# Forgetting attention with a feed-forward network on one core: exponentials transposed in 32 by 32 blocks by VectorE and carried across partitions by wide DMAs, in place of TensorE transposes

## The chip, the cores and the metric

The kernel runs on one core of a Trainium2 chip. The metric is the time of the core in microseconds (us), from the first to the last instruction and what lies around them. Engines: TensorE (PE, with its weight loads PEld), VectorE (DVE), ScalarE (ACT), GpSimd (POOL), SyncE (SP), whose queue issues all DMAs here. SBUF is the working memory with 128 partitions, PSUM the eight banks that TensorE writes.

## The reference, cut to what matters

```python
scores = scale * np.matmul(q, k.transpose(0, 1, 3, 2))       # q, k, v: 8 batches, 8 heads, 576 tokens, 64
cum = np.cumsum(np.log(np.clip(f, 0.0001, 1.0)), axis=-1)
decay = cum[:, :, :, None] - cum[:, :, None, :]
scores = np.where(causal, -1000000000.0, scores + decay)     # causal: above the diagonal
attn = np.exp(scores - np.max(scores, axis=-1, keepdims=True))
attn = attn / (np.sum(attn, axis=-1, keepdims=True) + 1e-09)
x = np.matmul(attn, v)                    # then tokens by heads: 4608 x 512
h = x @ w_in                              # 512 x 2048
out = np.maximum(0.01 * h, h) @ w_out     # 2048 x 512
```

All is float32. The kernel gets float32 precision by splitting each operand into a high part, rounded to the type fp32r that TensorE multiplies in one pass, and a low part, the rest.

## The kernel before, in words

A first stage, called early here, handles the first 256 tokens of batches 0, 1 and 2 and loads and splits the weights of the feed-forward network. Then comes the main loop over 64 tasks, one a head: batches 3, 4, 5, 6, 7 whole (tasks 0 to 39, all 576 rows; "whole heads"), then the remaining rows 256 to 575 of batches 0, 1 and 2 (tasks 40 to 63; "short heads").

A head is worked in row blocks i = 0 to 4 (a short one in blocks 2 to 4). `scores` multiplies the split q and k (tiles s1, s2 stationary, m1, m2 moving, into PSUM banks `sc`), VectorE adds the causal mask and takes the row maximum (L425), ScalarE takes the exponential with the row sum (L431) into tile z of the block. The exponentials then stand with rows on partitions, but the product with v needs the columns there. One head later, `transposes` turns each 128-column piece by a TensorE matmul against the identity (L447) into PSUM `tr`; ScalarE rounds it to the high part `ph` (L460), VectorE subtracts to the low part `pl` (L462). `values` multiplies with the split v (`vs`, L489), adds the two halves of the result (L496, L497) into x. For each pair of heads, `inverse` takes reciprocals of the row sums, turns them on TensorE and spreads them over partitions through DRAM (`inv`, `rb`); `normalise` multiplies x by them (L530) and writes x to the DRAM tensor `xd`.

The feed-forward network takes groups of 256 tokens from `xd` as they become ready. It is a generator, `ffn`, which yields after each quantum of TensorE work: 12 matmuls of the first product (L576, banks `h`) or 6 of the second (L614, banks `o0`, `o1`); 576 quanta in all. `fill(step)` draws quanta between the parts of a head, so that TensorE works on them while the other engines handle scores; `step` is set from the quanta available (`have`) and the tasks left until the next batch is ready. The activated g is rounded on VectorE (L589) and its low part taken on GpSimd (L140).

The order of each engine's instructions is mostly that of a scheduler that moves instructions by its own estimates; only those given to `keep_in_program_order` keep the written order. Semaphores tie the engines; tiles of one tag share buffers, so a later one waits for the readers of an earlier one.

Of the kernel before, what the change touches and what calls it, by code (L numbers as in the profile page):

```python
# [16 lines left out]
P = 128  # L17
DELAY = 3
ORDER = (3, 4, 5, 6, 7, 0, 1, 2)
HP = 4  # L20
# [3 lines left out]
B2 = 7  # L24
# [9 lines left out]
ZE = (("z0", "z1", "z2", "z3"), ("vm", "s2b", "m2b", "s2a"))  # L34
# [3 lines left out]
WARM = (20, 2)  # L38
NEG = -1.0e30
REBIAS = 2.0**-112  # L40


@with_exitstack
def forgetting_attention_ffn(ctx, tc, qT, kT, v4, vr, f, w_in, w_out, out):
# [6 lines left out]
    nc = tc.nc  # L51
# [8 lines left out]
    STEP = (P + REST) // 2  # L60
    ST = [*range(0, (NFULL - 1) * P + 1, P)]
    ST.append(ST[-1] + STEP)
# [5 lines left out]
    PST = S - P  # L68
    PT0 = NFULL * PST + STEP
    PTW = PT0 + P  # L70
# [7 lines left out]
    def rows(i):  # L78
        return P if i < NFULL - 1 else STEP

    def width(i):
        return ST[i] + rows(i)

# [35 lines left out]
    make_identity(nc, eye)  # L119
# [72 lines left out]
    def decays():  # L192
# [8 lines left out]
        d = one.tile([P, P + T], F32, tag="z3", name="d")  # L201
        for i in range(2):
            n = width(i)
# [31 lines left out]
    def load(t):  # L235
# [4 lines left out]
        for name, src, lo in (("q", qT, a), ("k", kT, 0)):  # L240
            x = h[name] = one.tile([P, S], F32, tag=f"{name}raw", name=f"{name}raw_{t}")
            for o in range(2):
                nc.sync.dma_start(x[o * D:(o + 1) * D, lo:n], src[s][:, lo:n])
        if s % 2 == 0:
# [4 lines left out]
            pairs[s // 2, c0] = dict(vm=vm)  # L249

    early = {}

    def early_load(b, g):

        e = early[b, g] = {}
        x = e["qk"] = one.tile([P, 2, T], F32, tag="b2", name=f"qk_{b}_{g}", bufs=B2)
# [4 lines left out]
        v = e["v"] = one.tile([P, 2, T // P, D], F32, tag="b2", name=f"ve_{b}_{g}", bufs=B2)  # L261
        nc.sync.dma_start(v, v4[b * HPB // 2 + g][:, :, :T // P])

    def early_split(b, g, mx, sm):
# [13 lines left out]
        for i in range(2):  # L278
            n, at = width(i), i * P
# [20 lines left out]
    def early_scores(b, g):  # L300
# [38 lines left out]
    def early_values(b, g):  # L339
        e = early[b, g]  # L340
        out = psum.tile([P, 512], F32, tag="tr", name=f"ave_{b}_{g}")
        for o in range(2):
# [5 lines left out]
            pt = one.tile([P, 3 * P], F32, tag=("z4", "m2a")[o], name=f"pte_{b}_{g}_{o}")  # L348
# [15 lines left out]
    def fix():  # L364

        for x in "ab":
# [4 lines left out]
            y = fixed["sum" + x] = one.tile([P, NCH, 2], F32, tag="sum" + x, name=f"fixed_sum{x}")  # L371
            nc.gpsimd.memset(y, 1.0)
        for i in range(NFULL - 1, NCH):
            z = fixed[f"z{i}"] = one.tile([P, (i + 1) * P], F32, tag=f"z{i}", name=f"fixed_z{i}")
            nc.gpsimd.memset(z, 0.0)
        vs = fixed["vs"] = one.tile([P, 2, NCH, 2 * D], F32R, tag="vs", name="fixed_vs")
        vm = fixed["vm"] = one.tile([P, 2, NCH, D], F32, tag="vm", name="fixed_vm")
        nc.gpsimd.memset(vm[:, :, NFULL], 0.0)

    def split(t):  # L380
# [5 lines left out]
        x = "ab"[t % 2]  # L386
        s1 = h["s1"] = one.tile([P, S], F32R, tag="s1", name=f"s1_{t}", bufs=1)
        m1 = h["m1"] = one.tile([P, S], F32R, tag="m1", name=f"m1_{t}", bufs=1)
        s2, m2 = h["s2"], h["m2"] = fixed["s2" + x], fixed["m2" + x]
        nc.scalar.copy(s1[:, a:n], h["q"][:, a:n])  # L390
        nc.scalar.copy(m1[:, :n], h["k"][:, :n])
        nc.sync.dma_start(s2[D:, a:n].bitcast(F32), s1[D:, a:n].bitcast(F32))
        nc.sync.dma_start(s2[2:4, a:n].bitcast(F32), dec_q[s][:, a:n])
        nc.sync.dma_start(m2[:2, :n].bitcast(F32), dec_k[s][:, :n])
        minus(s1[:D, a:n], h["q"][:D, a:n], s1[:D, a:n].bitcast(F32))
        minus(m2[D:, :n], h["k"][D:, :n], m1[D:, :n].bitcast(F32))
# [362 lines left out]
```

## Time and profile before

| | |
|---|---|
| median of 3 runs | 1197.04 us (1196.57 to 1198.4) |
| profiled execution | 1197.86 us, its span 1196.1 us |
| PE, PEld busy | 99%, 88% |
| DVE, ACT, POOL busy | 49%, 53%, 36% |
| DMA | 110.48 MB, 30.4% of 16 engines |
| granted TensorE clock | 1.0 |

In rows of groups the columns are the line, engine, operation, tiles written and read, shapes and count, then busy us in all, mean ns of one, and the engine's idle time before with what ended it. In rows by time they are start, length, engine, line. In rows by stretch they are length, then busy time and instructions of each engine, TensorE's clock, the DMA engines' share and GB/s. A row of one line's instructions gives minimum, median and maximum in ns. Records of matmuls overlap, since they are pipelined.

### The profile page before, as it was taken

The numbers are of one execution on the slowest core, as the hardware profiler recorded it, in microseconds if no ns is written. First come the engines' busy times: TensorE is split into PE (matmuls) and PEld (weight loads), VectorE is DVE, ScalarE is ACT, GpSimd is POOL, SyncE is SP. The second block draws the span as 40 slices with busy tenths as digits, with TensorE's granted clock in tenths as the row PEclk, the third lists the DMA queues.
The fourth block names the chain that finished last, engine by engine and source line by source line (L and its number), as shares of the span: only waits on it lengthen the run. The fifth ranks groups of instructions, "written<-read, shape, count | busy, mean of one in ns | idle before, by whom it ended". The sixth has DMA issues, their size and how long they took to land.

```text
span 1196.1 us, 21843 instructions
## 1 busy us (share of the span) xinstructions
PE 1178.5 (99%) x7876; PEld 1050.5 (88%) x7876; DVE 581.3 (49%) x1561; ACT 636.2 (53%) x1531; POOL 436.6 (36%) x347
## 2 busy tenths in 40 slices
PE   9999999999999999999999999999999999999998
PEld 6777888989999989999989999999999899888987
DVE  6888655644545455444454354433343445552221
ACT  7877666755565555555565454433444556652111
POOL 1001534444535344444444443434343444441000
PEclk9999999999999999999999999999999999999999
DMA  7555333333233323333222223122212233321000
GB/s 235 192 182 187 88 118 98 92 115 89 80 99 98 116 68 92 98 106 86 73 87 91 88 67 100 48 76 74 76 55 88 69 101 100 90 69 55 11 18 18
DMA packets 75819, 110.48 MB, mean 92 GB/s; under 512 B 14464, under 2 KB 45424, under 8 KB 75712
## 3 DMA queue, kind: packets, MB, share of 16 engines
q1 hardware_dynamic: 75712, 109.09, 30.4%
q8 instruction: 62, 1.02, 0.3%
q14 instruction: 45, 0.37, 0.1%
HBM read 82.62 MB, written 18.56 MB: 85 GB/s over the span
## 4 chain that ended last, share of the span: by engine, by line
PE 89%; DVE 4%; ACT 3%; issue 2%; POOL 1%; DMA 0%; SPq 0%; DVEq 0%; ACTq 0%; POOLq 0%
PE h L576 32%; PE o L614 31%; PE av L489 8%; PE sc L420 8%; PE tr L447 6%; PE warm L115 1%; DVE wt L170 1%; POOL xs L140 1%; PE ave L351 1%; PE sce L313 1%; ACT ze L296 1%; ACT wt L167 1%; PE tre L345 0%; DVE fixed_z L425 0%; DMA rb<-inv 0%
## 5 line engine op out<-in xcount | busy, mean ns | idle before, releaser
L576 PE MATMUL h<-xh,win_h 128*128 128x256 f32 x1152 | 326.6, 284 | 0.8 <-DVE xh L548 0.8
L576 PE MATMUL h<-xh,win_l 128*128 128x256 f32 x1152 | 323.2, 281 | 0.0
L576 PE MATMUL h<-xs,win_h 128*128 128x256 f32 x1024 | 287.0, 280 | 4.6 <-POOL xs L140 4.6
L140 POOL TENSOR_TENSOR gl<-g,gh 128x512 fp32r<-128x512 f32 x116 | 150.3, 1296 | 319.7 <-DVE gh L589 297.1
L614 PE MATMUL o<-wout_h,gh 128*128 128x512 f32 x576 | 232.8, 404 | 0.0
L614 PE MATMUL o<-wout_l,gh 128*128 128x512 f32 x576 | 229.1, 398 | 0.0
L614 PE MATMUL o<-wout_h,gl 128*128 128x512 f32 x576 | 228.0, 396 | 0.0
L576 PEld LDWEIGHTS h<-xh,win_h 128*128 128x128 f32 x1152 | 217.1, 189 | 7.0 <-DVE xh L548 1.2
L576 PEld LDWEIGHTS h<-xh,win_l 128*128 128x128 f32 x1152 | 216.9, 188 | 0.3 <-issue 0.2
L583 ACT ACTIVATE g<-h 128x512 f32<-128x512 f32 x144 | 85.6, 594 | 220.3 <-PE h L576 219.9
L576 PEld LDWEIGHTS h<-xs,win_h 128*128 128x128 f32 x1024 | 193.0, 188 | 9.9 <-POOL xs L140 6.0
L460 ACT CAST ph<-tr 128x128 fp32r<-128x128 f32 (+2 forms) x272 | 121.7, 449 | 123.5 <-PE tr L447 120.6
L589 DVE CAST gh<-g 128x512 fp32r<-128x512 f32 x144 | 80.2, 557 | 218.1 <-ACT g L583 214.8
L140 POOL TENSOR_TENSOR s<-qraw,s 64x576 fp32r<-64x576 f32 (+1 forms) x64 | 78.9, 1233 | 268.2 <-ACT s L390 264.9
L462 DVE TENSOR_TENSOR pl<-tr,ph 128x128 fp32r<-128x128 f32 (+2 forms) x272 | 138.2, 516 | 42.5 <-ACT ph L460 42.4
L425 DVE CUSTOM_DVE_ANT_0 z<-sc,tri 128x128 f32<-128x128 f32 (+1 forms) x144 | 63.7, 444 | 142.0 <-PE sc L420 141.0
L614 PEld LDWEIGHTS o<-wout_h,gl 128*128 128x128 f32 x576 | 108.4, 188 | 24.6
L614 PEld LDWEIGHTS o<-wout_h,gh 128*128 128x128 f32 x576 | 108.7, 189 | 16.8 <-issue 0.2
L614 PEld LDWEIGHTS o<-wout_l,gh 128*128 128x128 f32 x576 | 108.7, 189 | 15.7
L420 PE MATMUL sc<-m,s 128*128 128x128 f32 (+2 forms) x336 | 121.6, 367 | 0.1
L431 ACT ACTIVATE fixed_z<-fixed_z,max 96x480 f32<-96x480 f32 (+1 forms) x128 | 94.3, 737 | 43.8 <-DVE max L425 42.5
L425 DVE CUSTOM_DVE_ANT_0 fixed_z<-sc,tri 96x480 f32<-96x480 f32 (+1 forms) x128 | 70.4, 550 | 75.9 <-PE sc L420 75.1
(129 smaller groups left out, 1826.5 us busy)
## 6 DMA issues: line engine op xcount, KB each, us to landing
kraw<-in_kT SPq DMA_DIRECT2D x128, 144.0 KB
qraw<-in_qT SPq DMA_DIRECT2D x80, 144.0 KB
wraw<-in_w_in SPq DMA_DIRECT2D x16, 512.0 KB
wraw<-in_w_out SPq DMA_DIRECT2D x16, 512.0 KB
fixed_vm<-in_v SPq DMA_DIRECT2D x32, 256.0 KB
xs<-xd SPq DMA_DIRECT2D x16, 512.0 KB
out<-ost SPq DMA_DIRECT2D x28, 256.0 KB
rb<-inv SPq DMA_DIRECT2D x40, 144.0 KB
```

The source lines that it names most:

```text
L140: nc.gpsimd.tensor_tensor(out, a, b, op=ALU.subtract)
L420: nc.tensor.matmul(ps[:m, :b - a], h["s" + w][:, cols], h["m" + w][:, a:b], start=y == 0, stop=y == 1,)
L425: nc.vector.tensor_tensor_reduce(out=z[:, a:b], in0=ps[:m, :b - a], in1=tri[:m, at:at + b - a], scale=-SCALE, scalar=3.0e38 if x == 0 else ...
L431: nc.scalar.activation(z, z, AF.Exp, bias=h["max"][:m, last:last + 1], scale=-1.0, accum_out=fixed["sum" + "ab"[s // 2 % 2]][:m, i, s % 2: ...
L447: nc.tensor.transpose(ps[:, x * m:(x + 1) * m], z[:m, j * P:(j + 1) * P], ident[:m, :m])
L460: nc.scalar.copy(o, src)
L462: nc.vector.tensor_tensor(o, src, hi.bitcast(F32), op=ALU.subtract)
L489: nc.tensor.matmul(ps[:, a - lo:hi - lo], fixed["vs"][:, odd, j, :], h[w][:, at:at + hi - a], start=(n == 0), stop=(n == len(steps) - 1),)
L576: nc.tensor.matmul(ph[:, e, :], w[:, c, fs], xx[:, c, :], start=(c == 0 and x == 0), stop=(c == NCC - 1 and x == 2),)
L583: nc.scalar.activation(g, ph, AF.Prelu, alpha=0.01)
L589: nc.vector.tensor_copy(gh, g)
L614: nc.tensor.matmul(acc[k], gg[:, e, ts], w[:, e, :], start=(fc_ == 2 * p0 and x == 0), stop=(fc_ == 2 * p1 - 1 and x == 2),)
```

## The change

The TensorE transposes go. VectorE transposes each block's exponentials within 32 by 32 squares (`turn`, eleven instructions a whole head) into a collecting tile `zt`. What is left of the transposition is a permutation of groups of 32 partitions: `send` writes `zt` to a DRAM tensor `zd` by DMAs of 32 partitions each (four after block 2 and four after block 4; four in a short head), and in the next head `receive` reads it back by one DMA of 128 partitions into `pl`. `divide` rounds it to `ph` on ScalarE and leaves the low part in `pl` on VectorE, in two halves. `values` runs two heads after `scores`. Row blocks now end at multiples of 128 counted from row 64, so that the first has 64 rows; the columns of `values` are in a permuted token order, which `segments` undoes when the output is written.

Beside this: s2 and m2 are made by `prepare`, with ScalarE casting the upper halves, in place of a DMA that copied a half of s1; loads run two heads ahead; `inverse` and its spreading are apart; g has 5 buffers in place of 7 and a yield moves ahead of its rounding; and from the main loop on, all five engines keep the written order (`Lanes`). With `LEAD`, the first tasks draw at least 7 quanta each while fewer than 48 are used. Every call now passes through one helper, so that most instructions bear one line number.

The diff, cut to its core:

```diff
-B2 = 7
+LEAD = 7
+B2 = 5
+        def issue(*args, **kw):
+            ins = f(*args, **kw)
+            if self.on[0]:
+                self.tc.keep_in_program_order(ins)
+            return ins
...
-    ST = [*range(0, (NFULL - 1) * P + 1, P)]
-    ST.append(ST[-1] + STEP)
+    ST = [0, *range(REST, S, P)]
+    Q = 32
+    FW, PW = 15 * Q, 12 * Q
...
+    def prepare(t):
...
+        for y, x, lo in ((s2, h["q"], a), (m2, h["k"], 0)):
+            nc.scalar.copy(y[D:, lo:n], x[D:, lo:n])
+        minus(h["q"][D:, a:n], h["q"][D:, a:n], s2[D:, a:n].bitcast(F32))
+        minus(m2[D:, :n], h["k"][D:, :n], m2[D:, :n].bitcast(F32))
...
-        nc.sync.dma_start(s2[D:, a:n].bitcast(F32), s1[D:, a:n].bitcast(F32))
...
-    def transposes(t, i):
-        for x, j in enumerate(blocks_):
-            nc.tensor.transpose(
-                ps[:, x * m:(x + 1) * m], z[:m, j * P:(j + 1) * P], ident[:m, :m]
-            )
...
+    def turn(t, i):
...
+            nc.vector.transpose(
+                ap(zt[0][:m], base + u * Q, *dims), z[:, js[0] * P:(js[-1] + 1) * P]
+            )
+        base, w, u = unit(t, i, i)
+        nc.vector.transpose(ap(zt[0][:m], base + u * Q, [w, 2]), z[:, i * P:i * P + 2 * Q])
+
+    def send(t, part):
...
+        src = src.rearrange("p (b c) -> p b c", b=4)
+        for a in range(4):
+            to = zd[t % 2][a, :, lo:hi].rearrange("(b i) c -> i b c", b=4)
+            nc.sync.dma_start(to, src[a * Q:(a + 1) * Q])
+
+    def receive(t):
+        w = PW if tasks[t][1] else FW
+        zq = state[t]["pl"] = one.tile([P, 4 * FW], F32R, tag="pl", name=f"pl_{t}")
+        y = zd[t % 2][:, :, :w].rearrange("a p c -> p a c")
+        nc.sync.dma_start(zq[:, :4 * w].bitcast(F32).rearrange("p (a c) -> p a c", a=4), y)
+
+    def divide(t, half):
...
+        z, ph = h["pl"][:, c], h["ph"][:, c]
+        nc.scalar.copy(ph, z.bitcast(F32))
+        nc.vector.tensor_tensor(z, z.bitcast(F32), ph.bitcast(F32), op=ALU.subtract)
...
                 nc.scalar.activation(g, ph, AF.Prelu, alpha=0.01)
+                yield True
                 gh = one.tile([P, 2, T], F32R, tag="b2", name=f"gh_{n}_{p}", bufs=B2)
...
-                yield True
                 if pending is not None:
...
+    for t in range(nt + 2):
+        if t < nt:
+            load_v(t)
...
         step = min(have / (left + SLACK), MAXQ) / 8
-        fill(step)
+        if used[0] < 3 * HP * (2 + T // P):
+            step = max(step, LEAD / 8)
         for i in range(5):
-            if i in before:
-                transposes(t - 1, i)
             if i in now:
                 scores(t, i)
+            if i - 1 in now:
+                spread(t, i - 1)
+            if old is not None and i == 0:
+                divide(old, 1)
+            if i == 0 and 0 < t <= nt and tasks[t - 1][0] % 2:
+                spread_inverse(t - 1)
+            if i == 1 and t + 1 < nt:
+                prepare(t + 1)
             fill(step)
+            if old is not None and i == 2:
+                values(old, 0)
...
+            if i == 2 and 0 < t <= nt:
+                receive(t - 1)
...
+                    add(old, part)
+                if s % 2:
+                    normalise(old)
...
+        if t + 2 < nt:
+            load(t + 2)
+        if t < nt:
+            spread(t, 4)
+            if tasks[t][0] % 2:
+                inverse(t)
+        fill(step)
+        if t < nt:
+            split_v(t)
+        fill(step)
+        if 0 < t <= nt:
+            divide(t - 1, 0)
+        fill(step)
```

How the order moves, at three places in the whole heads. First SyncE's queue over one head without an inverse; before (`fixed_s2`, `fixed_m2` are s2 and m2, `dec_q` and `dec_k` their decay rows in DRAM; the names end in the head and a number):

```order
L521 DMA rb_19_5243<-inv_126 64x576 x2
L393 DMA fixed_s2a_1527<-dec_q_128 2x576
L392 DMA fixed_s2b_1535<-s1_21_5352 64x576
L243 DMA qraw_22_5376<-in_qT 64x576 x2
L243 DMA kraw_22_5379<-in_kT 64x576 x2
L247 DMA fixed_vm_1548<-in_v4 128x2x256
L532 DMA xd_125<-x_18_5113 128x576
L248 DMA fixed_vm_1548<-in_vr 64x2x64
L394 DMA fixed_m2a_1530<-dec_k_127 2x576
```

And now:

```order
L54 DMA xs_6_5136<-xd_125 128x4x256
L54 DMA fixed_s2a_1466<-dec_q_130 2x576
L54 DMA fixed_m2a_1469<-dec_k_129 2x576
L54 DMA pl_20_5215<-zd_0_127 128x4x480
L54 DMA zd_1_128<-zt_1482 32x4x192 x4
L54 DMA xd_125<-x_18_5006 128x576
L54 DMA qraw_23_5271<-in_qT 64x576 x2
L54 DMA kraw_23_5274<-in_kT 64x576 x2
L54 DMA zd_1_128<-zt_1482 32x4x288 x4
```

The copy of a half of s1 is gone; the receive stands ahead of the first four sends of the head itself, and the loads, now for two heads later, stand between the two groups of sends.

Then VectorE from block 2 to block 4 of one head; before (ISA rows with `sc` are the mask and maximum, those without are the read of the maximum):

```order
L425 ISA z2_17_4639,max_17_4592<-sc_17_2_0_4640,tri_141 128x384
L425 ISA max_17_4592 128x1
L462 TENSOR_TENSOR pl_16_4586<-tr_16_2_4633,ph_16_4585 128x3x128
L425 ISA fixed_z3_1543,max_17_4592<-sc_17_3_0_4658,tri_141 96x480
L425 ISA max_17_4592 96x1
L462 TENSOR_TENSOR pl_16_4586<-tr_16_3_4651,ph_16_4585 128x4x96
L425 ISA fixed_z4_1545,max_17_4592<-sc_17_4_0_4684,tri_141 96x288
L425 ISA max_17_4592 96x1
L462 TENSOR_TENSOR pl_16_4586<-tr_16_4_4676,ph_16_4585 128x5x96
L425 ISA fixed_z4_1545,max_17_4592<-sc_17_4_1_4688,tri_141,max_17_4592 96x288
L425 ISA max_17_4592 96x1
```

And now:

```order
L54 ISA z3_21_5217,max_21_5128<-sc_21_3_0_5218,tri_144 128x448
L54 ISA max_21_5128 128x1
L54 STREAM_TRANSPOSE zt_1482<-z2_21_5178 128x2x4x32
L54 STREAM_TRANSPOSE zt_1482<-z2_21_5178 128x2x32
L54 TENSOR_TENSOR x_18_5006<-av_19_0_5197,y_19_5208 64x512
L54 TENSOR_TENSOR x_18_5006<-av_19_1_5210,yz_19_5213 64x64
L54 TENSOR_TENSOR x_18_5006<-x_18_5006,rb_19_4952 128x512
L54 TENSOR_TENSOR x_18_5006<-x_18_5006,rb_19_4952 128x64
L54 ISA z4_21_5241,max_21_5128<-sc_21_4_0_5242,tri_144 128x288
L54 ISA max_21_5128 128x1
L54 ISA z4_21_5241,max_21_5128<-sc_21_4_1_5246,tri_144,max_21_5128 128x288
L54 ISA max_21_5128 128x1
```

The subtraction out of `tr` after each block has become block transposes of the block before; two additions of the values two heads older stand between blocks 3 and 4, and, in every second head, the normalisation.

Last TensorE around the values of one head; before:

```order
L447 MATMUL tr_20_4_5493<-ident_r_91,fixed_z4_1545 128x96 x5
L420 MATMUL sc_21_4_0_5501<-m1_21_5353,s1_21_5352 96x288
L420 MATMUL sc_21_4_0_5501<-fixed_m2b_1538,fixed_s2b_1535 96x288
L420 MATMUL sc_21_4_1_5505<-m1_21_5353,s1_21_5352 96x288
L420 MATMUL sc_21_4_1_5505<-fixed_m2b_1538,fixed_s2b_1535 96x288
L614 MATMUL o_5_0_0_5128<-wout_h_4_113,gh_5_4_5398 128x512
L489 MATMUL av_20_0_5511<-ph_20_5402,fixed_vs_1547 128x448 x2
L489 MATMUL av_20_0_5511<-ph_20_5402,fixed_vs_1547 128x320
L489 MATMUL av_20_0_5511<-ph_20_5402,fixed_vs_1547 128x192
L489 MATMUL av_20_0_5511<-ph_20_5402,fixed_vs_1547 128x64
```

And now:

```order
L54 MATMUL o_5_0_0_5190<-wout_h_0_109,gl_5_0_5101 128x512
L54 MATMUL av_19_0_5197<-ph_19_5114,fixed_vs_1484 128x512 x2
L54 MATMUL av_19_0_5197<-ph_19_5114,fixed_vs_1484 128x4x96
L54 MATMUL av_19_0_5197<-ph_19_5114,fixed_vs_1484 128x4x64
L54 MATMUL av_19_0_5197<-ph_19_5114,fixed_vs_1484 128x4x32
L54 MATMUL av_19_0_5197<-pl_19_5025,fixed_vs_1484 128x512 x2
L54 MATMUL av_19_0_5197<-pl_19_5025,fixed_vs_1484 128x4x96
L54 MATMUL av_19_0_5197<-pl_19_5025,fixed_vs_1484 128x4x64
L54 MATMUL av_19_0_5197<-pl_19_5025,fixed_vs_1484 128x4x32
L54 MATMUL av_19_1_5210<-ph_19_5114,fixed_vs_1484 128x64
L54 MATMUL av_19_1_5210<-pl_19_5025,fixed_vs_1484 128x64
L54 MATMUL sc_21_3_0_5218<-m1_21_5064,s1_21_5063 128x448
```

The transposes ahead of the scores are gone, and the values, of two heads before, stand between the scores of blocks 2 and 3, one whole accumulation after the other.

More of the change, by code (lines that the diff above doesn't have):

```diff
@@ L429, in scores @@
             )
+        if i == NCH - 1 and t + 1 < nt:
+            split(t + 1)
         last = i + len(parts) - 1
@@ L474, in values @@
+    def divide(t, half):
+        h = state[t]
+        w = 2 * (PW if tasks[t][1] else FW)
+        if not half:
+            h["ph"] = one.tile([P, 4 * FW], F32R, tag="ph", name=f"ph_{t}")
+        c = slice(half * w, (half + 1) * w)
+        z, ph = h["pl"][:, c], h["ph"][:, c]
+        nc.scalar.copy(ph, z.bitcast(F32))
+        nc.vector.tensor_tensor(z, z.bitcast(F32), ph.bitcast(F32), op=ALU.subtract)
     def values(t, part):
@@ L494, in values @@
         other = slice(D - odd * D, 2 * D - odd * D)
-        y = one.tile([P, 512], F32, tag="y", name=f"y_{t}_{part}")
-        nc.scalar.copy(y[mine, :hi - lo], ps[other, :hi - lo])
-        nc.vector.tensor_tensor(
-            x[mine, lo:hi], ps[mine, :hi - lo], y[mine, :hi - lo], op=ALU.add
-        )
+        tag = "yz" if part else "y"
+        y = one.tile([P, n], F32, tag=tag, name=f"{tag}_{t}")
+        nc.scalar.copy(y[mine], ps[other, :n])
+        h["add", part] = x[mine, at:at + n], ps[mine, :n], y[mine]
@@ L523, in normalise @@
+        rb = pairs[s // 2, c0]["r"] = one.tile([P, NCH * P], F32, tag="part0", name=f"rb_{t}")
+        for o in range(2):
+            y = inv[s // 2, o, :m * P]
+            y = bass.AP(tensor=y.tensor, offset=y.offset, ap=[[0, D], *y.ap])
+            nc.sync.dma_start(rb[o * D:(o + 1) * D, :m * P], y)
     def normalise(t):
@@ L600, in ffn @@
                         split_group(m)
[L601 removed]
+                if p0 <= p < p1 - 1 and at + 1 < len(order):
                     fetch_group(order[at + 1][0])
@@ L690, in forgetting_attention_ffn, with spread @@
     fix()
-    beside[0] = True
+    beside[0] = ordered[0] = True
     load(0)
+    prepare(0)
     split(0)
-    for t in range(nt + 1):
-        if t + 1 < nt:
-            load(t + 1)
-        before = list(range(*tasks[t - 1][1:])) if t else []
+    def spread(t, i):
+        if tasks[t][1] and not tasks[t - 1][1] and i == 2:
+            nc.gpsimd.memset(zt[0][:, :4 * PW], 0.0)
+        turn(t, i)
+        if i == 4 or i == 2 and not tasks[t][1]:
+            send(t, i // 4)
+    load(1)
@@ L703, in forgetting_attention_ffn @@
         for i in range(5):
-            if i in before:
-                transposes(t - 1, i)
             if i in now:
                 scores(t, i)
-            fill(step)
-            if t and i == 1 and tasks[t - 1][0] % 2:
-                inverse(t - 1)
-        if t:
-            for part in range(len(spans(t - 1))):
-                values(t - 1, part)
-                fill(step)
-            if tasks[t - 1][0] % 2:
-                normalise(t - 1)
-            s, c0, c1 = tasks[t - 1]
-            if s % HPB == HPB - 1:
-                ready[0] = place[s // HPB, c0 * P] + width(c1 - 1) - c0 * P
@@ new lines, in forgetting_attention_ffn @@
+            if old is not None and i == 2 and not tasks[old][1]:
+                values(old, 1)
+            if i == 2 and 0 < t <= nt:
+                receive(t - 1)
+            if old is not None and i == 3:
+                s, c0, c1 = tasks[old]
+                for part in range(1 if c0 else 2):
+                    add(old, part)
+                if s % 2:
+                    normalise(old)
+                if s % HPB == HPB - 1:
+                    ready[0] = place[s // HPB, c0 * P] + S - c0 * P
```

302 lines of the change are left out of this document (186 added, 116 removed).

## The prediction

> **What bounds the kernel now.** I read the page first, for the engine shares, the slices and the chain.
>
> ```profile
> span 1196.1 us, 21843 instructions
> PE 1178.5 (99%) x7876; PEld 1050.5 (88%) x7876; DVE 581.3 (49%) x1561; ACT 636.2 (53%) x1531; POOL 436.6 (36%) x347
> ...
> PEclk9999999999999999999999999999999999999999
> DMA  7555333333233323333222223122212233321000
> GB/s 235 192 182 187 88 118 98 92 115 89 80 99 98 116 68 92 98 106 86 73 87 91 88 67 100 48 76 74 76 55 88 69 101 100 90 69 55 11 18 18
> ...
> PE 89%; DVE 4%; ACT 3%; issue 2%; POOL 1%; DMA 0%; SPq 0%; DVEq 0%; ACTq 0%; POOLq 0%
> PE h L576 32%; PE o L614 31%; PE av L489 8%; PE sc L420 8%; PE tr L447 6%; PE warm L115 1%; DVE wt L170 1%; POOL xs L140 1%; PE ave L351 1%; PE sce L313 1%; ACT ze L296 1%; ACT wt L167 1%; PE tre L345 0%; DVE fixed_z L425 0%; DMA rb<-inv 0%
> ```
>
> TensorE is busy for 99% of the span at full clock, and 89% of the chain is TensorE itself. So its work is the time: the feed-forward lines L576 and L614 hold 63%, and the attention's values (L489), scores (L420) and transposes (L447) hold 22%. Nothing else is near its limit over the span, and the DMA slices fall from 7 to 2 or 3 tenths after the first few.
>
> Next I cut the span by heads (first score matmul of heads 2, 10, 18, 34, 40, 50, 58 and 63; heads 0 to 39 are whole, 40 to 63 short).
>
> ```profile
> core 0: us, PE busy (x) PEld busy (x) DVE busy (x) ACT busy (x) POOL busy (x), PEclk, DMA share, GB/s
> 148.60:258.90 110.30, 106.51 (x738) 96.61 (x737) 62.35 (x180) 67.89 (x175) 47.60 (x37) 1.00 0.37 109
> 258.90:385.10 126.20, 125.16 (x859) 113.61 (x858) 64.93 (x182) 72.86 (x183) 59.11 (x42) 1.00 0.32 94
> 385.10:647.30 262.20, 262.15 (x1792) 239.06 (x1791) 127.50 (x365) 147.96 (x369) 115.08 (x85) 1.00 0.31 90
> ...
> 1070.50:1196.10 125.60, 120.41 (x773) 107.47 (x771) 29.20 (x59) 21.64 (x41) 7.34 (x4) 1.00 0.08 24
> ```
>
> From head 10 on TensorE never waits. In heads 2 to 9 it idles 3.8 of 110.3 us. The 16 heads of the third row take 16.4 us each, of which VectorE works 8.0, ScalarE 9.2 and GpSimd 7.2; at 90 GB/s the DMAs carry 1.5 MB a head. So VectorE and ScalarE have 7 to 8 us a head to spare.
>
> The matmuls overlap in the records, so their cost is read from start to start, in a stretch of one head:
>
> ```profile
> 500.25 0.28 PE L576 MATMUL h<-xh,win_l 128*128 128x256 f32 x1
> 500.37 0.49 PE L447 MATMUL tr<-ident_r,z 128*128 128x128 f32 x3
> 500.62 0.42 PE L420 MATMUL sc<-m,s 128*128 128x384 f32 x1
> ...
> 501.05 0.40 PE L614 MATMUL o<-wout_h,gh 128*128 128x512 f32 x1
> 501.29 0.40 PE L614 MATMUL o<-wout_l,gh 128*128 128x512 f32 x1
> ...
> 502.46 0.50 PE L447 MATMUL tr<-ident_r,fixed_z 96*128 96x96 f32 x4
> 502.74 0.44 PE L420 MATMUL sc<-m,s 128*96 128x480 f32 x1
> ...
> 504.63 0.58 PE L447 MATMUL tr<-ident_r,fixed_z 96*128 96x96 f32 x5
> 504.99 0.35 PE L420 MATMUL sc<-m,s 128*96 128x288 f32 x1
> ...
> 506.98 0.85 PE L489 MATMUL av<-ph,fixed_vs 128*128 128x448 f32 x5
> ...
> 508.45 0.36 PE L576 MATMUL h<-xh,win_h 128*128 128x256 f32 x1
> ```
>
> A feed-forward matmul of 256 columns costs 0.12 us, one of 512 costs 0.24: about 0.46 ns a column. A quantum of the interleaving (12 of the former or 6 of the latter) is 1.4 us.
>
> **The change, part by part.**
>
> *TensorE, transposes.* Three transposes take 0.25 us (500.37 to 500.62), four 0.28, five 0.36: 0.89 us for twelve, 74 ns each. With
>
> ```profile
> L447 PE MATMUL tr<-ident_r,fixed_z 96*128 96x96 f32 x576 | 68.6, 246 | 0.0
> L447 PE MATMUL tr<-ident_r,z 128*128 128x128 f32 x312 | 57.7, 273 | 0.0
> ```
>
> 888 x 74 ns = 66 us go. The chain's 6% (72 us) is the upper end, the cheapest of the three (four in 0.28 us, 62 us) the lower.
>
> *TensorE, scores.* The new row blocks give 2 x 1600 score columns a whole head in place of 2 x 1824, and 2 x 1344 in place of 2 x 1440 in a short one: 40 x 448 + 24 x 192 = 22,500 columns fewer, at 0.46 ns 10 us; the narrowest gain less, so I take 9.
>
> *TensorE, values.* They grow, since blocks are computed in units of 128 columns whether or not the causal edge needs them: 3712 columns a whole head against 3200, 3072 against 2432 in a short one, 35,800 more in all. The old ones run at (508.45 - 506.98) / 2944 = 0.50 ns a column: 18 us; at the feed-forward rate 16. I take 17. Whether reading four strided segments is slower than one run no row shows; I take no extra cost, 0 to 10 us.
>
> TensorE's work falls by 66 + 9 - 17 = 58 us.
>
> *VectorE.* A whole head loses the five low-part subtractions out of PSUM and gains eleven block transposes (1600 columns) and two subtractions of 960 columns with both operands in SBUF.
>
> ```profile
> L462 DVE TENSOR_TENSOR pl<-tr,ph 128x384 fp32r<-128x384 f32 x128 | 69.4, 551 | 3.0 <-ACT ph L460 2.9
> L530 DVE TENSOR_TENSOR x<-x,rb 128x576 f32<-128x576 f32 x20 | 22.8, 1142 | 2.4 <-DMA rb<-inv 1.7
> L530 DVE TENSOR_TENSOR x<-x,rb x32: 491/759/1693, 170.7 to 1086.7; 128x576 f32<-128x576 f32 x20, 128x320 f32<-128x320 f32 x12
> L589 DVE CAST gh<-g x144: 371/428/2279, 50.2 to 1187.5; 128x512 fp32r<-128x512 f32 x144
> ```
>
> The old subtractions are 1824 columns at 551/384 = 1.43 ns: 2.6 us. The new ones, by the 759 ns that 576 columns take undisturbed (1.04 ns a column and 0.16 us), are 1.16 us each; the same row reaches 1693, and the larger form has a mean of 1142, so 1.5 us each and 3.1 a head. No row shows a block transpose. The fastest VectorE copy (371 ns for 512) would make 1600 columns 1.2 us, the dearest row (1693 for 576) 4.7; nearest is an undisturbed fp32 operation between SBUF tiles, 1.04 ns a column and 0.16 us an instruction: 3.4 us. VectorE goes from 8.0 to 8.0 - 2.6 + 3.1 + 3.4 = 11.9 us a whole head (9.7 to 13.2). Heads that take 14 us cover this.
>
> If each new subtraction waits as long as the worst of the row (934 ns more), VectorE needs 8.0 - 2.6 + 4.2 + 3.4 = 13.0 us. [...]
>
> *ScalarE.* The copies out of PSUM become two of 960 columns out of SBUF, about even; two casts of 64x576 are added in place of a DMA.
>
> ```profile
> L391 ACT CAST m<-kraw 128x576 fp32r<-128x576 f32 x64 | 43.2, 674 | 0.0
> ```
>
> 2 x 0.67 us: 9.2 becomes 10.5 us a whole head, covered by TensorE.
>
> *SyncE's queue.* Each DMA costs issue time there, one after the other, and in written order.
>
> ```profile
> L243 SPq DMA_DIRECT2D kraw<-in_kT x128: 465/587/748, 105.7 to 1058.8; - x128
> L392 SPq DMA_DIRECT2D fixed_s2a<-s x32: 488/514/528, 120.3 to 1055.5; - x32
> L515 SPq DMA_DIRECT2D inv<-rt x64: 644/712/805, 161.9 to 1081.4; - x64
> L521 SPq DMA_DIRECT2D rb<-inv x64: 477/544/1472, 165.6 to 1083.6; - x64
> L521 SPq EVENT_SEMAPHORE  x33: 17/988/1007, 165.5 to 1082.1; - x33
> L247 SPq DMA_DIRECT2D fixed_vm<-in_v x32: 572/574/1593, 118.2 to 1050.0; - x32
> L394 SPq DMA_DIRECT2D fixed_m2b<-dec_k x32: 223/428/436, 124.0 to 1054.6; - x32
> ```
>
> Per whole head now: four loads 4 x 0.57 = 2.3; two decay rows 0.9; half a pair's v, inverse and x, (0.57 + 0.57 + 2 x 0.71 + 2 x 0.54 + 0.54) / 2 = 2.1; out and xs 0.5; with gaps 6 us. The change removes the duplicate of s1 (0.5) and adds eight sends and a receive. A send is nearest to L392, which also starts from part of the partitions: 8 x 0.51 + 0.54 = 4.6; bounds 8 x 0.43 and 8 x 0.71. Gaps of 50 ns for 20 DMAs add 1.0. That makes 11.4 us a whole head (10.8 to 13.0), plus the wait for the landed inverse (0.99 us a pair, behind which everything on the queue waits) and other waits in order: the receive waits for values two heads older, a load for the split of the head before. I take 12.8 us. A short head has four sends and needs under 10.
>
> *DMA traffic.* A whole head adds 0.98 MB each way and drops 0.15: 1.5 becomes 3.3 MB, in 14.5 us 228 GB/s. The first slice moves 235 GB/s at share 0.7, so the engines carry about 330; it fits, with latency. What is late next is the low half of the division: the receive follows values(t-2) in the third step of five and its tile is wanted four fills later, 6 to 7 us; 0.98 MB at 300 GB/s is 3.3 us, and queue and landing add about 2. Behind a late division stand, on ScalarE and VectorE, the next head's exponentials and block maxima, and behind those TensorE's score banks.
>
> *Heads 2 to 9.* A head's own matmuls take (262 - 129 x 1.4) / 16 = 5.1 us now (the order has 129 quanta in heads 18 to 33), 4.0 after the transposes are gone. Only the early groups feed TensorE until the first batch is ready, and the new order gives heads 2 to 9 33 quanta instead of 46. TensorE then has 33 x 1.4 + 8 x 4.0 = 78 us of work, while the queue needs 8 x 12.8 = 103 and VectorE 8 x 11.9 less one cast = 92. The stage takes 103; 25 us idle in place of 3.8: +21 us. The other 13 quanta run elsewhere and are in the total.
>
> *Other heads.* Heads 10 to 17 have seven quanta, 13.8 us, heads 18 to 33 7.8, 14.9 us, against 12.8 on the queue and 11.9 on VectorE, all in fixed order: I give them 8 us of idle, bounds 0 and 45. Heads 34 to 39 (9.5 quanta, 17.3 us) and the short ones have slack.
>
> *End.* The last values come two heads later: five quanta (7 us) stand between values 62 and 63, the chain of receive, two divisions and values needs about 9: +2.
>
> *Costed at nothing.* The g tiles fall from seven buffers to five and the rounding of g moves a quantum later: four quanta (5.6 us) still lie between it and its first reader, against 0.4 us for the cast and 1.3 for GpSimd. The early stage changes tiles, not work; 3 us either way.
>
> Sum: -58 + 21 + 8 + 2 = -27 us. The profiled execution took 1197.9 (span 1196.1 and 1.8 around it), so 1171; the median of the runs is 0.8 lower: 1170.
>
> **The rivals.**
> 1. *Queue and VectorE keep up everywhere.* Heads 2 to 9 then idle as they do now and the others not at all: 1197 - 58 + 2 = 1141, with 5 us of stalls 1146 (1132 to 1155). For it: 7 us of slack a head on both compute engines now. Against it: 33 quanta in eight heads.
> 2. *SyncE's queue sets the time of the whole heads, and the kernel is slower.* Heads 2 to 33 take 103 + 8 x 13.8 + 16 x 14.9 + 8 = 460 us in my sum, 14.4 each. If the in-order waits stretch the queue's round to 16 us, they take 512: +52, 1222. From 15.2 us a head on (27 us over 32 heads) the change loses. For it: 20 issues at 0.4 to 0.7 us in fixed order, with waits for landings between. Against it: the landing wait now is 1 us a pair.
> 3. *A block transpose costs four times my price.* At 4.2 ns a column it takes 8.4 us a head, VectorE 16.9: 32 x 2.5 us more, 1251. It decides from 6.7 us a head on. No row excludes it.
> 4. *No relief.* TensorE's idle grows by what its work loses: within 0.2% (2.4 us, about what a measurement of this kernel can tell from no change) of 1197, or a little beside it.
>
> **How the numbers follow.** My forecast (1155 to 1188) has 0.47, rival 1 0.21, rival 2 0.18 (spread from 1188 to 1245), rival 3 0.07, rival 4 0.07. Faster are the first two, a seventh of rival 2 and a seventh of rival 4: 0.72. Rival 4 gives 0.05 for no change and rival 2 0.01; the rest, 0.22, is slower. The range leaves out the upper half of rival 2, rival 3 and the lowest tenth of rival 1: 1136 to 1216.
>
> **What would show it.** In the changed profile: no transposes beyond the early ones, TensorE's busy time down some 55 to 60 us plus idle in heads 2 to 9 ended by VectorE; block transposes of 128x128 near 0.3 us; SyncE issuing 20 DMAs a whole head in 11 to 13 us; heads 10 to 17 near 14 us. Wrong would be: sends of 0.8 us or more, waits of ScalarE for the received tile in most heads, or values matmuls over 0.6 ns a column.

## The result, and the profile after

The change made the kernel slower: 1283.38 us (1279.95 to 1291.57) against 1197.11, a ratio of 1.073 (95% interval 1.068 to 1.078). The forecast was 1170, with 1136 to 1216 as its range; both its sign and its range were wrong. The profiled execution took 1279.95 us. Its page, with the groups that are new or wait most:

```profile
span 1277.9 us, 21528 instructions
PE 1146.4 (90%) x6988; PEld 1014.7 (79%) x6988; DVE 735.2 (58%) x2045; ACT 694.3 (54%) x1515; POOL 439.8 (34%) x347
...
PEclk9999888799999999999999999999998979889998
DMA  6563566677766667676776566565666646640000
...
PE 48%; DMA 22%; DVE 10%; ACT 8%; issue 6%; SPq 4%; POOL 1%; DVEq 0%; ACTq 0%; POOLq 0%
PE h L54 17%; DMA pl<-zd 16%; PE o L54 16%; PE av L54 6%; SPq L54 4%; PE sc L54 4%; ACT ph L54 3%; DMA inv<-rt 2%; DVE zt L54 2%; DMA zd<-zt 2%; ACT z L54 2%; DVE z L54 2%; DVE pl L54 2%; PE ave L54 1%; PE sce L54 1%
...
L54 ACT CAST ph<-pl 128x960 fp32r<-128x960 f32 (+1 forms) x128 | 116.9, 928 | 129.1 <-DMA pl<-zd 129.1
```

TensorE's busy time fell, but it no longer fills the span: 90% in place of 99%. The chain of work that ended last is TensorE for 48% in place of 89%, and a DMA for 22%, of which the receive (`pl<-zd`) alone is 16%. ScalarE waits 129 us for that tile before its casts. The clock row, all nines before, has sevens and eights.

The waits of TensorE that end in a group (total us, times, longest us):

```profile
PE sc L54 <- DVE max L54: 36.2, 25, 7.3
PE av L54 <- ACT ph L54: 36.0, 11, 10.3
PE rt L54 <- DVE r L54: 28.9, 18, 2.8
```

And the stages, cut as before by the first score matmul of a head (heads 2, 10, 18, 34, 40, 50, then 63 to the end):

```profile
core 0: us, PE busy (x) PEld busy (x) DVE busy (x) ACT busy (x) POOL busy (x), PEclk, DMA share, GB/s
158.60:282.60 124.00, 91.81 (x497) 81.34 (x495) 76.30 (x234) 70.89 (x160) 42.69 (x33) 0.86 0.67 202
282.60:405.80 123.20, 111.33 (x700) 100.45 (x700) 80.45 (x248) 78.40 (x174) 51.45 (x39) 0.99 0.69 206
405.80:669.50 263.70, 241.78 (x1520) 218.30 (x1521) 176.07 (x510) 159.34 (x354) 115.57 (x85) 0.98 0.69 206
...
1118.30:1277.90 159.60, 138.82 (x850) 124.39 (x849) 36.99 (x72) 25.86 (x46) 11.40 (x7) 0.94 0.15 43
```

Heads 2 to 9 idle for 32 us of 124 (3.8 of 110 before), heads 18 to 33 for 22 of 264 (none before).

For the comparison of all versions I add up each profiled execution from TensorE's records and its clock: time in which a matmul runs, less what the reduced clock took of it (half of the busy time that lies in stretches granted 0.5), is *work*; that loss is *clock*; time between matmuls is *gaps*; the time after the last matmul is *end*. A constant 1.5 us ahead of the first matmul is left out. The four parts add up to the span of the profiled execution and not to the median; in inverse_late that execution was, at 1267.8 us, near the slowest.

| kernel | median us | work | clock | gaps | end |
|---|---|---|---|---|---|
| before | 1197.11 | 1178.5 | 0 | 12.4 | 3.7 |
| after | 1283.38 | 1108.0 | 38.3 | 118.2 | 11.8 |
| out_pieces | 1241.85 | 1109.2 | 28.9 | 94.0 | 5.1 |
| inverse_late | 1261.01 | 1111.8 | 36.8 | 103.8 | 12.1 |
| both | 1220.68 | 1112.1 | 21.1 | 77.4 | 5.1 |
| inverse_last | 1217.43 | 1115.2 | 24.2 | 67.9 | 5.2 |
| low_later | 1204.79 | 1113.6 | 18.2 | 63.4 | 5.1 |
| inverse_apart | 1182.33 | 1112.9 | 13.2 | 47.5 | 5.5 |

From before to after, work fell by 70.5 us, more than the 58 forecast. Gaps grew by 105.8, the clock took 38.3 and the end 8.1, together 152.2; less the 70.5, that is 81.7, the difference of the spans. So the removal worked, and the question is where the waits come from.

### The profile page after: what moved, and what is told of

The parts are those of the page before. It is cut to its first block, busy times and chain, and to the rows that moved or that the text cites. A ratio compares the mean times of both kernels' runs of the same rounds, so it can differ in the third digit from the quotient of the medians.

```text
span 1277.9 us, 21528 instructions
## 1 busy us (share of the span) xinstructions
PE 1146.4 (90%) x6988; PEld 1014.7 (79%) x6988; DVE 735.2 (58%) x2045; ACT 694.3 (54%) x1515; POOL 439.8 (34%) x347
## 4 chain that ended last, share of the span: by engine, by line
PE 48%; DMA 22%; DVE 10%; ACT 8%; issue 6%; SPq 4%; POOL 1%; DVEq 0%; ACTq 0%; POOLq 0%
PE h L54 17%; DMA pl<-zd 16%; PE o L54 16%; PE av L54 6%; SPq L54 4%; PE sc L54 4%; ACT ph L54 3%; DMA inv<-rt 2%; DVE zt L54 2%; DMA zd<-zt 2%; ACT z L54 2%; DVE z L54 2%; DVE pl L54 2%; PE ave L54 1%; PE sce L54 1%
## 5 line engine op out<-in xcount | busy, mean ns | idle before, releaser
L54 DVE TENSOR_TENSOR pl<-pl,ph 128x960 fp32r<-128x960 f32 (+1 forms) x128 | 149.2, 1175 | 226.7 <-ACT ph L54 226.4
L54 ACT ACTIVATE z<-z,max 64x64 f32<-64x64 f32 (+3 forms) x272 | 160.9, 592 | 214.2 <-DVE max L54 211.5
L54 POOL TENSOR_TENSOR gl<-g,gh 128x512 fp32r<-128x512 f32 x116 | 158.3, 1364 | 270.3 <-DVE gh L54 193.0
L54 PEld LDWEIGHTS h<-xh,win_h 128*128 128x128 f32 x1152 | 222.7, 193 | 5.5 <-ACT xh L54 0.9
L54 PEld LDWEIGHTS h<-xh,win_l 128*128 128x128 f32 x1152 | 222.7, 193 | 0.1
L54 DVE CUSTOM_DVE_ANT_0 z<-sc,tri 64x64 f32<-64x64 f32 (+3 forms) x272 | 122.0, 449 | 127.0 <-PE sc L54 120.3
L54 ACT CAST ph<-pl 128x960 fp32r<-128x960 f32 (+1 forms) x128 | 116.9, 928 | 129.1 <-DMA pl<-zd 129.1
L54 DVE STREAM_TRANSPOSE zt<-z 128x64 f32<-128x64 f32 (+5 forms) x608 | 167.3, 317 | 29.6 <-ACT z L54 28.3
L54 ACT ACTIVATE g<-h 128x512 f32<-128x512 f32 x144 | 85.4, 593 | 133.3 <-PE h L54 129.1
L54 PE MATMUL sc<-m,s 128*128 128x64 f32 (+2 forms) x336 | 109.4, 331 | 41.3 <-DVE max L54 36.2
L54 PE MATMUL av<-ph,fixed_vs 128*128 128x512 f32 (+3 forms) x360 | 77.2, 334 | 36.0 <-ACT ph L54 36.0
```

The costliest lines, as they stand in the source:

```text
L54: ins = f(*args, **kw)
```

## The experiments

**Two suspects of the changed kernel.** The first is the output write. In the permuted token order a block of 128 rows no longer goes to 128 rows that follow each other; the change writes it in one to three DMAs, and of these 57 DMAs 31 have a DRAM side of 2 blocks of 32 rows and 8 one of 4. At the end of the kernel the last of these writes, each of 2 blocks, run with nothing beside them; then the end of the kernel before:

```profile
1268.60:1276.60 8.00, 0.00 (x0) 0.00 (x0) 0.00 (x0) 0.00 (x0) 0.00 (x0) 0.50 0.13 44
```

```profile
1193.10:1195.50 2.40, 0.00 (x0) 0.00 (x0) 0.00 (x0) 0.00 (x0) 0.00 (x0) 1.00 0.35 131
```

No engine computes in either. The share of 0.13 for 8 us is the time of two DMA engines of 16 (2/16), at 44 GB/s; before, the writes move at 131 GB/s and a share of 0.35. In mid-kernel, this is SyncE's queue around four writes of 2 blocks (start, length), then the same time by stretches, and the receive as a piece of the chain:

```profile
721.94 2.75 SPq L54 DMA_DIRECT2D out<-ost  x4
724.73 3.16 SPq L54 DMA_DIRECT2D xs<-xd  x1
728.00 0.66 SPq L54 DMA_DIRECT2D fixed_s2a<-dec_q  x1
728.70 2.12 SPq L54 DMA_DIRECT2D fixed_m2a<-dec_k  x1
730.93 0.38 SPq L54 DMA_DIRECT2D pl<-zd  x1
```

```profile
722.00:724.00 2.00, 2.00 (x14) 1.78 (x13) 0.69 (x3) 1.21 (x3) 0.00 (x0) 1.00 0.67 200
724.00:728.00 4.00, 4.00 (x27) 3.59 (x26) 2.77 (x9) 2.60 (x7) 1.96 (x2) 1.00 0.13 32
```

```profile
730.93 10.66 DMA pl<-zd
```

For four us the DMA engines move 32 GB/s at share 0.13, while the queue stands in the issue of the next wide transfer (3.16 us); the receive behind it takes 10.66 us, where its landings in undisturbed whole heads, worked out from the semaphore events, take 5.0 to 6.0. These rows show the share of 0.13 beside writes whose slowest dimension is 2; that the form causes it, they do not show, and the runs below test it.

The second suspect is the place of `spread_inverse`: in the odd heads its two reads wait on the queue until the inverse has landed, in front of the receive, and its transpose makes TensorE wait for VectorE (28.9 us above).

*out_pieces:*

```diff
-                    y = out[row:row + m, :]
-                    if times > 1:
-                        y = bass.AP(tensor=y.tensor, offset=y.offset, ap=[[far * DM, times], *y.ap])
-                    nc.sync.dma_start(y, o[x:x + m * times])
+                    for k_ in range(times):
+                        nc.sync.dma_start(
+                            out[row + k_ * far:row + k_ * far + m, :], o[x + k_ * m:x + (k_ + 1) * m]
+                        )
```

> Theory A, few-engine writes: the output writes of the changed kernel have a DRAM side of [2 or 4][32][512], run at about 30 GB/s, and every wide transfer issued after them waits behind them; then 32-row writes of their own end this, no receive takes over 7 us to land because of them, and the time falls by 30 to 55 us, to 1230-1255. Theory B, the queue's order: the receive is late because it is issued late; then the time falls by under 10 us, and the extra issues (some 100 at 0.5 us) may even cost. Theory C, VectorE and the fixed order: no change within 5 us.

Measured: 1241.85 us, ratio to before 1.037 (1.0345 to 1.0395): 41.5 us less, although SyncE issues 55 DMAs more. Gaps fall by 24, the clock's loss by 9, the end by 7. Receives that land after more than 7 us, by the same working, fall from 14 to 7 of 64, the longest from 13.5 to 9.0 us, and ScalarE's wait for them from 129.1 to 91.1 us. The same rows still go to the same places, so it was the form of the DMA and not the scattered rows. Theory A holds; what makes the seven receives that are left late, no run shows.

*inverse_late:*

```diff
-            if i == 0 and 0 < t <= nt and tasks[t - 1][0] % 2:
-                spread_inverse(t - 1)
...
                 receive(t - 1)
+            if i == 3 and 0 < t <= nt and tasks[t - 1][0] % 2:
+                spread_inverse(t - 1)
```

> The spreading of the inverse moves from the first step of the next head to the fourth, behind the receive. Theory B: in odd heads the receive is issued 3 to 4 us sooner and TensorE no longer waits for the reciprocal (28 us in the changed kernel), so the time falls by 25 to 45 us, to 1240-1260. Theory A: at most 10 us. Theory C: the 28 us of waits for the reciprocal move to the next wait for VectorE, no change within 5 us.

Measured: 1261.01 us, 1.053 (1.051 to 1.055): 22.4 us less, just short of what theory B said and over twice what the others allowed. Of the theory's two parts one came true: ScalarE's wait for the receive fell from 129.1 to 76.2 us. The transpose's wait for VectorE only changed its name, from the reciprocal (28.9 us) to the additions (24.0), and the queue even waits longer for the landed inverse (80.6 us in place of 52.1 in the changed kernel), now with the receive ahead of it.

*both:* the two edits together.

> The two edits together. If A and B both hold and their waits are different ones, the falls add up: 55 to 90 us, to 1195-1230, near the kernel before. If they end the same waits, it is within 10 us of the better of the two. Theory C: still over 1265.

Measured: 1220.68 us, 1.020 (1.018 to 1.021): 62.7 us less, and the single falls add up to 63.9. They are two causes.

*no_receive:*

```diff
...
-        zq = state[t]["pl"] = one.tile([P, 4 * FW], F32R, tag="pl", name=f"pl_{t}")
-        y = zd[t % 2][:, :, :w].rearrange("a p c -> p a c")
-        nc.sync.dma_start(zq[:, :4 * w].bitcast(F32).rearrange("p (a c) -> p a c", a=4), y)
+        state[t]["pl"] = fixed["pl"]
...
```

> The receive is left out: divide works on a tile that was filled once, so the values are those of other data and no instruction waits for the transport; sends, block transposes, divisions and products stay. If transport (A or B) is what costs, TensorE's idle falls from 115 to under 40 us and its clock stays high: 1150-1190. If VectorE or the fixed order costs (C), the time stays over 1235.

Measured: 1211.40 us, 1.011 (1.0075 to 1.014). Without the receive 72 us go, so the transport is where most of the loss reaches TensorE; but the time lies between the two expectations. Gaps are still 64 us, 35.8 of them at the transpose of the reciprocals. Not all of it is transport.

```profile
PE rt L54 <- DVE r L54: 35.8, 17, 8.2
```

**The form of the write by itself, in the kernel before.** *before_two* gave its output writes a DRAM side of two halves that follow each other:

```diff
-                    nc.sync.dma_start(out[row:row + m, :], o[x:x + m])
+                    y = out[row:row + m, :]
+                    y = bass.AP(tensor=y.tensor, offset=y.offset, ap=[[m // 2 * DM, 2], [DM, m // 2], [1, DM]])
+                    nc.sync.dma_start(y, o[x:x + m])
```

> The kernel before, with each of its output writes given a DRAM side of [2][rows/2][512], nothing else. Theory A in its narrow form, that a write on few engines costs only where TensorE waits for a transfer behind it: loads here run a head ahead, so 1197 to 1203. In its wide form, that it delays all that follows by some 10 us: every batch of loads behind a write comes late, 1215 or more. Rival, that the form of the write has nothing to do with its speed: unchanged, and the writes land as fast as before.

Measured: 1197.30 us, 1.000 (0.999 to 1.001). This says nothing of A: the two dimensions were merged again when the kernel was built, and in the records the writes have 128 rows as before. *before_permuted* therefore took `ap=[[DM, 2], [2 * DM, m // 2], [1, DM]]`, which can't merge.

> The kernel before, with each output write given a DRAM side of [2][rows/2][512] that can't be merged (rows of the block go out in the order 0, 2, 4 .. 1, 3, 5 .., so they land permuted); in before_two the two halves followed each other and the access pattern folded back to the old one. Theory A, narrow: the writes then land after 8 us or more in place of 2 to 4, loads behind them come up to 10 us late, but a head ahead of their use: 1197 to 1205. Wide: 1215 or more. Rival, the form of the write does not matter: they land in 2 to 4 us and the time is 1197.

Measured: 1243.77 us, 1.039 (1.037 to 1.042): 47 us slower, by the form of 40 DMAs alone. Its end, in which nothing but the last two writes runs, and the longest pieces of its chain in time that are no matmuls:

```profile
1228.00:1232.00 4.00, 0.00 (x0) 0.00 (x0) 0.00 (x0) 0.00 (x0) 0.00 (x0) 0.71 0.13 47
1232.00:1236.00 4.00, 0.00 (x0) 0.00 (x0) 0.00 (x0) 0.00 (x0) 0.00 (x0) 0.50 0.13 51
```

```profile
158.67 11.61 DMA out<-part
208.88 6.27 DMA fixed_s2a<-s
555.45 8.71 DMA fixed_s2a<-s
990.67 8.07 DMA fixed_s2a<-s
1069.13 8.78 DMA inv<-rt
```

Again the share of two engines; and the small DMA that hands a half of s1 to s2, on TensorE's path there, takes 6 to 9 us behind such a write. In the kernel before none of its 64 takes over 3.4 us, by the semaphore events. Theory A holds in its wide form: what waits behind the write comes late, and in this kernel, too, somebody needs it.

**What is left after both edits.** In *both*, TensorE waits in these places:

```profile
PE rt L54 <- DVE x L54: 25.5, 20, 2.5
PE sc L54 <- DVE max L54: 22.6, 21, 3.6
PE av L54 <- ACT ph L54: 16.3, 11, 2.5
```

*inverse_last* moves `spread_inverse(t - 1)` on to the end of the fifth step (`if i == 4`, after the additions).

> Output writes in pieces, and the spreading of the inverse moved on to the end of the fifth step, behind the additions whose PSUM bank its transpose takes (in the version in the fourth step TensorE waited there 25.5 us for VectorE's additions). Theory D, waits of the fixed order add up on TensorE one by one: idle falls by some 20 us more and the time from 1221 to 1195-1205. Rival, VectorE is late as a whole and the wait only changes its name: within 5 us of 1221.

Measured: 1217.43 us, 1.017 (1.016 to 1.019), 3 us less. The rival was right: the wait changed its name.

```profile
PE sc L54 <- DVE max L54: 33.1, 31, 3.8
...
PE rt L54 <- DVE x L54: 3.7, 9, 0.7
```

*slack_1* is inverse_last with `SLACK = 1`.

> As inverse_last, with SLACK 1 in place of 3, so that heads 2 to 9 draw more of the feed-forward quanta that are there (of 60 left after the early stage some 55 in place of 47 by head 10). If heads 2 to 9 idle for want of quanta, their idle (22.8 us with both edits) falls by 8 to 12 us and the time by 8 to 15 us against inverse_last. Rival, they idle in waits of the chain whatever TensorE has: the work only moves and the time stays within 4 us.

Measured: 1232.93 us, 1.031 (1.029 to 1.032), 15.5 us slower than inverse_last. Heads 2 to 9 drew 41 quanta in place of 33 and took 113.4 us in place of 112.8, so eight quanta did fit into their waits; but the quanta are missing later, where TensorE now waits for a fresh group of tokens (inverse_last has no such rows):

```profile
PE h L54 <- POOL xs L54: 19.7, 6, 5.6
...
PE h L54 <- DVE xh L54: 13.9, 6, 4.7
```

*low_later*, on top of inverse_last, splits `divide`: the cast stays, the subtraction moves a step on.

```diff
+        h["low", half] = z, ph
+
+    def low(t, half):
+
+        z, ph = state[t]["low", half]
         nc.vector.tensor_tensor(z, z.bitcast(F32), ph.bitcast(F32), op=ALU.subtract)
...
             if old is not None and i == 0:
+                low(old, 0)
                 divide(old, 1)
+            if old is not None and i == 1:
+                low(old, 1)
```

> As inverse_last, with the subtraction of each half's low part issued one step after its cast, behind the next block's maximum and block transposes, so that VectorE does not wait at it for ScalarE (131 us with both edits). Theory D with VectorE in order as the cause of the waits for the row maximum (22.6 us): these fall by half or more, the time by 8 to 15 us against inverse_last. Rival: VectorE has 40% free, its wait covers nothing that TensorE needs, and the products now wait for the low part instead: within 4 us, or up to 5 us slower.

Measured: 1204.79 us, 1.006 (1.005 to 1.008), 12.6 us less, as theory D said, though the wait for the maximum falls by a little less than half, from 33.1 to 20.3 us:

```profile
PE sc L54 <- DVE max L54: 20.3, 16, 4.7
```

VectorE is busy 63% of the span and still cost time, because it stood in order at a subtraction whose operand ScalarE had just begun to make: its waits there fall from 144.8 to 62.9 us.

In the chain of low_later over heads 2 to 9 the DMA queue (12.9%) and the landing of the inverse (12.1%) come first, with the load of k close behind (12.0%). Three of the longer pieces:

```profile
198.90 3.86 DMA inv<-rt
205.85 3.34 DMA kraw<-in_kT
228.63 4.23 DMA inv<-rt
```

*inverse_apart*, on top of low_later, takes the reading back out of `spread_inverse`, into a function called one head later:

```diff
...
+    def read_inverse(t):
...
+            if old is not None and i == 1 and tasks[old][0] % 2:
+                read_inverse(old)
...
```

> As low_later, and the reading back of the inverse (two DMAs of 128 rows in all) is issued a head later, in front of the receive, in place of right behind its writing: so the DMA queue no longer stands still until the inverse has landed (2.2 to 4.2 us a pair in the chain of heads 2 to 9 of low_later), and the loads of q and k behind it go out that much sooner. Theory E, the landing wait at the head of the one queue is what still makes heads 2 to 9 idle: idle there falls from 22.8 to some 10 us, the time to 1185-1196, and it beats the kernel before. Rival, the heads' own chain (maximum, exponential, block transposes, divisions) sets them: within 5 us of 1205.

Measured: 1182.33 us, 0.988 (0.986 to 0.990): 22.5 us less than low_later, and faster than the kernel before. Its waits of the queue for the inverse fall from 43.2 to 2.6 us in all. Theory E holds, though the idle of heads 2 to 9 fell to 14.6 us and not to 10:

```profile
158.50:260.10 101.60, 87.00 (x498) 75.92 (x496) 72.56 (x235) 71.63 (x160) 43.81 (x33) 0.93 0.82 239
260.10:374.20 114.10, 109.84 (x700) 98.97 (x701) 82.90 (x248) 78.14 (x174) 54.92 (x39) 1.00 0.78 233
374.20:616.60 242.40, 237.46 (x1522) 214.12 (x1521) 171.96 (x510) 160.32 (x354) 120.14 (x85) 1.00 0.74 221
```

*apart_no_receive* makes the edit of no_receive there.

> As inverse_apart, without the receive (divide works on a tile filled once, the values are those of other data): what the transport still costs there. If the other edits have taken it off TensorE's path, within 8 us of inverse_apart. If each head still waits for its tile, 15 us or more below it.

Measured: 1165.44 us, 0.973 (0.972 to 0.975). So each head still waits for its tile: 16.9 us of the transport are on the path, where it was 72 in the changed kernel.

*order_free* is inverse_apart with `PINNED = ()`.

> As inverse_apart, with PINNED empty: the scheduler orders the five engines' instructions again, as in the kernel before, and only what keep_in_program_order names keeps its place. Theory F, the written order is a part of what the change costs: a scheduler would fill VectorE's and TensorE's waits, the time falls under 1175. Theory G, the written order pays for itself once its four bad places are mended: its spacing of receive, divisions and products is lost, and the time rises to 1190-1230. Between 1178 and 1187 it makes no difference.

Measured: 1502.49 us, 1.255 (1.253 to 1.257), far beyond what theory G said: TensorE busy 83%, clock 0.874, gaps 247 us. Neither theory had that. So the written order, which leaves all these waits in place, is at the same time worth 320 us against this scheduler's; which of its places does it was not tried.

## Why the prediction was wrong

- *Work.* Transposes, scores and values were to give 58 us; 70.5 went. Counted from each matmul's start to the next one's, without the gaps and with time at half clock halved, the transposes gave 63.5 us (66 said), the scores 14.9 (9), the values took 13.3 (17), and 5.7 more went in terms that I had not counted, the feed-forward matmuls and the reciprocals' transposes. Records overlap, so the split is rough (inverse_apart gives 18.7 for scores and 18.6 for values). Right in direction, and somewhat low.
- *Prices of the new operations.* Shown by these rows:

```profile
L54 DVE STREAM_TRANSPOSE zt<-z 128x128 f32<-128x128 f32 x104 | 29.5, 284 | 0.1
L54 DVE TENSOR_TENSOR pl<-pl,ph 128x960 fp32r<-128x960 f32 x80 | 97.9, 1225 | 146.0 <-ACT ph L54 146.0
...
L54 SPq DMA_DIRECT2D zd<-zt x416: 302/446/1778, 140.9 to 1137.0; - x139
```

  A block transpose of 128x128 takes 0.284 us (near 0.3 was said), a subtraction 1.23 (1.5; the 62 of 80 with no GpSimd work beside them have a median of 1.16, as said for an undisturbed one, and the 18 others one of 1.28 and a maximum of 2.25, so the longer times of the old row, for which I had taken 1.5, came in 9 of 80 alone, all over 1.39), a send 0.45 to issue (0.51). The old subtractions are 1632 columns a whole head by their rows, not the 1824 of the scores; that moves VectorE's sum by 0.1 us. VectorE needs 176.07 / 16 = 11.0 us a head in heads 18 to 33 (11.9), ScalarE 10.0 (10.5). Rival 3 is out.
- *The step that failed first: "out and xs 0.5".* I priced the output writes by their issue time and did not look at their new form. That is 41.5 us (out_pieces), and before_permuted shows such a cost, 47 us for 40 writes, without anything else of the change.
- *"Plus the wait for the landed inverse (0.99 us a pair ...)".* The wait itself was mis-sized a little (52.1 us over 32 in the changed kernel, 1.6 each). What was missed is what stands behind it, which the same sentence named and priced at 1.4 us a head with all other waits (12.8 for 11.4): the receive and the loads of q and k. In inverse_late the wait itself grew to 80.6 us and the kernel was still faster, because the receive no longer stood behind it. Its position cost 22.4 us (inverse_late) and, where the landing still stood ahead of the loads, another 22.5 (inverse_apart).
- *VectorE "covered".* I compared its 11.9 us with the 14 us of a head. Busy time was the wrong measure for an engine in written order; its wait for ScalarE's cast was not in the sum. Moving it gave 12.6 us.
- *Clock.* The sum had none. The gaps of TensorE in the changed kernel are paid about a third dearer than their length: 118.2 us of gaps and 38.3 of clock.
- *Heads.* I said 14.4 us a head in heads 2 to 33, and rival 2 gave 1222 if waits in order made it 16: it was (124.0 + 123.2 + 263.7) / 32 = 16.0. So rival 2 named the place and the size; I gave it 0.18, on the ground that the landing wait was 1 us a pair. Its mechanism, waits in order on SyncE's queue, is a part of what the runs showed: the form of the writes and VectorE's order were in no sum of mine. One sign of being wrong came as written: ScalarE waited for the received tile 35 times in 64 heads. The rest up to 1283 lies outside these heads: head 2 starts at 158.6 us in place of 148.6, and from head 34 to the end it is 608 us, where my sum left 561. In inverse_apart that last part is 564 us. The later start stays there (158.5): four quanta more are drawn in heads 0 and 1 (14 in place of 10, 5.6 us at 1.4), and TensorE idles 10.0 us in place of 5.6 before the first score, where I had put the early stage at nothing, "3 us either way".
- With the four places mended, the forecast's own stages come out: heads 2 to 33 take 458.1 us (460 was said), the kernel 1182 (1170). That the total comes so near is in part luck: against the kernel before, work fell by 65.6 us, 8 more than was said, which pays for a good half of the 13.2 us of clock that the sum had at nothing; gaps and end grew by 36.9 where 31 were said. What was left out of the sum was 101 us of waiting in order and behind writes at a share of 0.13, with the clock that such gaps cost, and not the price of an operation.

Three things stay open: the edits after *both* were measured on top of the earlier ones, so what each of them is worth by itself is not tested; no run touched the early stage; and how the 16.9 us left of the transport split between its latency and the bandwidth it takes from others.

## What to carry to other kernels

Where a change alters the order of rows or tokens, look at the shape of every DMA that it touches, not only at those it adds: one whose outermost dimension is 2 moved here at the share of two DMA engines (0.13), and what was issued behind it came late (a receive took 10.66 us in place of 5.0 to 6.0). On one in-order queue, price a wait by what stands behind it (22.4 and 22.5 us here); a write that is read back should be issued, then left for a while before the read. For an engine in written order, put other work between an operation and the reader of its result on another engine, even where its busy share says that it has time (12.6 us here).

## What the runs showed of the hardware beyond that

In the changed kernel the clock followed TensorE's idle time in stretches of 3.4 us: every record of half clock but the last, which the end cuts off, lasts 3.413 us or two, three or four times that. Four such stretches in a row, from 251.3 us on:

```profile
251.30:254.70 3.40, 3.40 (x21) 3.01 (x21) 3.16 (x9) 1.47 (x4) 1.30 (x1) 1.00 1.04 363
254.70:258.10 3.40, 1.46 (x14) 1.38 (x13) 3.13 (x11) 2.11 (x4) 0.87 (x1) 1.00 0.87 262
258.10:261.50 3.40, 3.40 (x16) 3.21 (x15) 1.95 (x7) 1.59 (x5) 0.00 (x0) 0.50 0.89 245
261.50:264.90 3.40, 3.40 (x20) 3.00 (x19) 1.84 (x7) 3.30 (x8) 2.14 (x2) 0.99 0.30 96
```

After a stretch with 1.94 us idle the next one is granted half the clock, and then the clock is back. In the changed kernel, by all its stretches of 3.41 us, every stretch of full clock with over 1.85 us idle was followed by one at half (18 of them, the least with 1.87), and none with less (the most 1.80); in inverse_apart the stretch from 208.8 to 212.2 us, with 1.87 us idle, was followed by one at half too. The way back was stricter: in the changed kernel full clock followed a stretch at half only when that one had at most 0.68 us idle, and eleven with 0.51 us or more were followed by another at half. So, as an estimate from these numbers, a gap of 2 us that falls into one stretch costs up to 1.7 us more, half of a stretch at half clock (3.41 / 2), if the next stretch is busy; one of 1 us, alone in its stretch, lies under the 1.80 us after which the clock stayed full here, and costs nothing more.
